# Luna attention and SMELU: first keys as float32 and cast on chip, values ahead of queries, softmax groups by halves of the heads

## The chip, the cores and the metric

The kernel runs on one core of a Trainium2 chip, in one launch. The metric is device time in microseconds, the median over runs; 260.56 us is the time before the change (3 runs, 260.14 to 262.5).

A core has five engines with a queue each: TensorE (PE, multiplies matrices into PSUM), VectorE (DVE), ScalarE (ACT), GpSimd (POOL) and SyncE (SP). Transfers are issued from the queues of SyncE, ScalarE and GpSimd. In this kernel those of GpSimd turn float32 in memory into bf16 on the way, those of the other two move data as it is, or transpose it.

## The reference

```python
batch, n_heads, seq, head_dim = (8, 8, 576, 64); n_pack = 32
def sm_attn(qq, kk, vv):
    s = scale * np.matmul(qq, kk.transpose(0, 1, 3, 2))      # scale = 1/sqrt(64)
    s = s - np.max(s, axis=-1, keepdims=True)
    a = np.exp(s)
    a = a / (np.sum(a, axis=-1, keepdims=True) + 1e-09)
    return np.matmul(a, vv)
p_packed = sm_attn(p, k, v)               # 32 packed rows for each head
out = sm_attn(q, p_packed, p_packed)      # 576 rows attend to the 32 packed rows
x = out, heads side by side               # (4608, 512)
h = x @ w_in                              # w_in (512, 2048)
g = where(h >= 1, h, where(h <= -1, 0, (h + 1)**2 / 4))
result = g @ w_out                        # w_out (2048, 512), float32
```

## The kernel before, in words

The work goes batch by batch, eight blocks. For a block, keys (`k`), queries (`q`) and values (`v`) are loaded as bf16 by GpSimd's queue (`load`, L251 to L255), two buffers of each. The stages of `attention`, by the names of its functions and tiles:

- `trans`: the tokens of four heads are transposed by 12 matmuls into `tp` (PSUM), and copied to `kT` or `qT` (SBUF). Blocks 3 to 7 use `turned` instead: a transposing transfer on SyncE's queue (L481).
- `scores`: `sp` = keys times packed queries for four heads, and `ex`, its exponential, on ScalarE. Two halves `i` = 0, 1.
- `packed`: `pk` = values times `ex` (48 small matmuls) and sums of `ex` (12), copied to `ppT`, in two layouts since a head is needed on the upper or lower 64 partitions; `rs` is the reciprocal of the sums.
- `weights(g)`: for a group `g` of four heads, `s2` = packed keys times queries, `eT` its exponential, `sm` the sums over the packed rows (a matmul with a block of ones), `ln` and `rc` (their reciprocal by logarithm and exponential) on ScalarE, and `A`, the normalised weights, on VectorE.
- `mk(f)`: `M` = packed values times a quarter of `w_in` (`mp` in PSUM), so that `h` below is `A` times `M`, without the attention's output being formed.
- `hidden_tile`: `h`, 4 matmuls each for 16 slices of the hidden layer; three steps on ScalarE and VectorE make the activation (`x`, and `hT` in bf16).
- `out_tile`: for two blocks at a time, nine tiles of 128 tokens; a tile is 16 matmuls (`o`) of `hT` with `w_out`, a copy to `ob`, and stores by SyncE's queue. Tiles 0 to 3 of a pair need the first block alone, so their `o` can be done while the second block's softmax is on its way.

Before the change a group `g` is every second head (`h` = 2a + g), so a group needs both halves of the queries. In the last tile of all (`done_last`) ScalarE and VectorE each copy half of the columns of one PSUM tile, and each half is stored by its own queue.

The order of instructions isn't written by hand. `Plan` (L31 to L172) replays the kernel at build time with a table of costs (`C`, L12 to L16): each task has engines that may do it, a cost, a key (its priority) and tasks that it depends on; `both` lets the planner choose between VectorE and ScalarE; PSUM tiles are rooms of which `W` has three and `O` two. The engine that can start first gets its next task, and the instructions are issued in that order. Each engine then runs its list in order and waits on semaphores. Until the first output tile has begun, TensorE is given dummy matmuls on a tile of zeros (L618, `idle`) wherever the planner sees it without work, each counted as `DW / 2400` us. Transfers of GpSimd's queue stand in the order in which they are added: keys in halves, queries, values, then four pairs of weight slices, then block 1, the rest of `p`, and from block 2 on as buffers come free.

Of the kernel before, what the change touches and what calls it, by code (L numbers as in the profile page):

```python
# [11 lines left out]
C = dict(load=3.0, w_in=2.65, w_out=2.55, out=9.0, p=3.1, land=1.9, xt=5.0, xland=2.5,  # L12
         tpp=0.06, tp=0.042, sc=0.034, pk=1.18, s2=0.25, sm=0.245, M=0.345, h=0.49, o=0.217, switch=0.05,
         pTc=0.1, Tca=1.12, Tcd=0.76, Tc2a=0.64, Tc2d=0.457, ex=0.82, ppTa=0.26, ppTd=0.293, rs=0.18, eT=0.74, ln=0.65, rc=0.68, A=0.82,
# [16 lines left out]
class Plan:  # L31
# [8 lines left out]
    def __init__(self, rooms):  # L40
        self.tasks, self.now, self.mode = [], {e: 0.0 for e in self.ENGINES}, 0
        self.rooms = {nm: [0.0] * n for nm, n in rooms.items()}
        self.count = {nm: 0 for nm in rooms}
        self.now["DMA"] = 2.85
        self.log = []
# [130 lines left out]
def kernel(  # L176
# [10 lines left out]
    nc = tc.nc  # L187
# [28 lines left out]
    nc.scalar.preload_act_table_set("natural_log_exp_and_others")  # L216

# [22 lines left out]
    nc.sync.dma_start(p_raw, p_v[:, :PB * 2])  # L240
# [10 lines left out]
    def load(nm, b, hs):  # L251
        if (nm, b) not in tok:
            tok[nm, b] = stg.tile([TP, H, NC, D], bf16, tag=nm, name=nm)
        nc.gpsimd.dma_start(tok[nm, b][:, hs].rearrange("p h c d -> p h (c d)"),  # L254
                            SRC[nm][b, hs].rearrange("h (p c) d -> p h (c d)", c=NC))  # L255
# [9 lines left out]
    nc.vector.memset(pT, 0.0)  # L265
    HS = [slice(0, 4), slice(4, 8)]
# [5 lines left out]
    def add_load(nm, b, parts=1, deps=()):  # L272
        for i, hs in enumerate([ALL] if parts == 1 else HS):
            L[nm, b, i] = add(DMA, C["load"] / parts, -1, deps, lambda nm=nm, b=b, hs=hs: load(nm, b, hs))
        if parts == 1:
            L[nm, b, 1] = L[nm, b, 0]
# [62 lines left out]

    def attention(b, key):  # L340
# [9 lines left out]
        def trans(nm, i, dst, prev):  # L350
# [11 lines left out]
            split = 2 if b == 0 else 1  # L362
            t = add(PE, C["tp"] * 12, ky, [L[nm, b, i]] + prev, mm, takes="W", readers=split, mode=0)
            if split == 1:
                def cp(eng):
                    w = 4 * E * TP
                    copy(dst()[:, i, :w].rearrange("p (j c) -> p j c", j=X), box["tp"][:, :, :w // 2])(eng)
                return t, [both(cp, C["Tca"], C["Tcd"], ky, [t], frees=t)]
            res = []
            for j in range(X):  # L370
                def cp(eng, j=j):
                    w = 2 * E * TP
                    copy(dst()[:, i, j * w:(j + 1) * w], box["tp"][:, j, :w])(eng)
                res.append(both(cp, C["Tc2a"], C["Tc2d"], ky, [t], frees=t))
            return t, res

        def scores(i, deps):
            box, ky = {}, key["sc" + str(i)]

            def mm():  # L380
                sp = box["sp"] = wide([P, 2, FW], f32, "sp")
                for j in range(2):
                    for e in range(E):
                        for g in range(G):
                            h, o = G * (2 * i + j) + g, (e * G + g) * X * NP
                            w = ((G * j + g) * E + e) * TP
                            nc.tensor.matmul(sp[:, j, o:o + X * NP], kT()[:, i, w:w + P],  # L387
                                             pT[:, b, h].rearrange("p x n -> p (x n)"), start=True, stop=True)

            def ev(eng):  # L390
                nc.scalar.activation(ex().rearrange("p e g x a n -> p a (e g x) n")[:, 2 * i:2 * i + 2],  # L391
                                     box["sp"][:TP, :, :E * G * X * NP].rearrange("p j (c n) -> p j c n", n=NP),
                                     AF.Exp, scale=scale)
            t = add(PE, C["sc"] * 12, ky, deps, mm, takes="W", readers=1, mode=0)
            return t, add(ACT, C["ex"], ky, [t] + old("pk"), ev, frees=t)

        def packed(deps):
            box, ky = {}, key["pk"]

            def mm():  # L400
# [3 lines left out]
                for a in range(Q):  # L404
                    for c in range(NC):
                        for g in range(G):
                            nc.tensor.matmul(v_[g * D:(g + 1) * D, a], vt[:, G * a + g, c], ex_[:, c // X, g, c % X, a],  # L407
                                             start=(c == 0), stop=(c == NC - 1))
# [5 lines left out]
            t = add(PE, C["pk"], ky, [L["v", b, 0]] + deps, mm, takes="W", readers=4, mode=1)  # L414
# [8 lines left out]
        def pp_of(x, g, a):  # L423
            return ppT()[x * D:(x + 1) * D, 0 if x == g else 1, a]

        def weights(g, deps, r):
            box, ky, km = {}, key["s2" + str(g)], key["sm" + str(g)]

            def mm():
                s2 = box["s2"] = wide([P, X, FW], f32, "s2")  # L430
                for a in range(Q):
                    for x in range(X):
                        nc.tensor.matmul(s2[a * NP:(a + 1) * NP, x, :HALF], pp_of(x, g, a),  # L433
                                         qT()[x * D:(x + 1) * D, a // 2, (G * (a % 2) + g) * E * TP:][:, :E * TP], start=True, stop=True)
# [31 lines left out]
        def mk(f, deps):  # L466
            box, ky = {}, key["M" + str(f)]

            def mm():
                mp = box["mp"] = wide([P, G, FW], f32, "mp")  # L470
                for a in range(Q):
                    for g in range(G):
                        nc.tensor.matmul(mp[a * NP:(a + 1) * NP, g], pp_of(g, g, a),  # L473
                                         w_in_sb[g * D:(g + 1) * D, a, f * FW:(f + 1) * FW], start=True, stop=True)
            t = add(PE, C["M"], ky, deps + [L["in", f]], mm, takes="W", readers=1, mode=2)
            return t, both(lambda eng: copy(M()[:, :, f * FW:(f + 1) * FW], box["mp"])(eng),
                           C["Mca"], C["Mcd"], ky, [t] + K.get((b - 2, "h"), []), frees=t)
# [19 lines left out]
        ws = [weights(g, pc + qc0 + qc1, r) for g in range(G)]  # L497
# [51 lines left out]
    def out_tile(pr, i):  # L549
        box, prev = {}, []  # L550
        bs = range(2 * pr + i * P // S, 2 * pr + ((i + 1) * P - 1) // S + 1)

        def step(fi):
            if fi == 0:
                box["o"] = psO.tile([P, d_model], f32, tag="o", name="o")
            nc.tensor.matmul(box["o"], hT[:, fi, i * P:(i + 1) * P], w_out_sb[:, fi, :], start=(fi == 0), stop=(fi == KF - 1))  # L556
# [7 lines left out]
        def done_last(eng):  # L564

            w = d_model // 2
            for j, (eng, queue) in enumerate(((ACT, nc.scalar), (DVE, nc.sync))):
                ob = ops.tile([P, w], f32, tag="ob" + str(j), name="ob" + str(j), bufs=1)
                copy(ob, box["o"][:, j * w:(j + 1) * w])(eng)
                for a, n, dst in out_rows(pr, i):  # L570
                    queue.dma_start(dst[:, j * w:(j + 1) * w], ob[a:a + n])
# [7 lines left out]
        both(done if 2 * pr + 2 < B or i + 1 < NT else done_last, C["oba"], C["obd"], b_key(pr, i), prev, frees=owner, takes="ob", holds=C["out"])  # L579
# [69 lines left out]
```

## Time and profile before

| | |
|---|---|
| median of the runs | 260.56 us |
| profiled execution, time | 261.9 us |
| its span | 259.8 us |
| granted TensorE clock, mean | 0.995 |
| busy: TensorE, ScalarE, VectorE | 247.3, 185.9, 173.3 us |
| busy: GpSimd | 27.4 us |
| moved by the DMA engines | 34.40 MB, mean 132 GB/s |
| GpSimd's queue (q0), SyncE's queue (q1) | 18.55 MB, 15.34 MB |

The span is from the first to the last instruction of one execution; its time has what lies around it too. Bytes are counted as they are written, so a load that casts counts half of what it reads. A busy share is a mean over stages with different limits: the first 23 us are loads and block 0's softmax, then blocks overlap until about 226 us, and the last 29 us are `o` alone.

### The profile page before, as it was taken

The numbers are of one execution on the slowest core, as the hardware profiler recorded it, in microseconds if no ns is written. First come the engines' busy times: TensorE is split into PE (matmuls) and PEld (weight loads), VectorE is DVE, ScalarE is ACT, GpSimd is POOL, SyncE is SP. The second block draws the span as 40 slices with busy tenths as digits, with TensorE's granted clock in tenths as the row PEclk, the third lists the DMA queues.
The fourth block names the chain that finished last, engine by engine and source line by source line (L and its number), as shares of the span: only waits on it lengthen the run. The fifth ranks groups of instructions, "written<-read, shape, count | busy, mean of one in ns | idle before, by whom it ended". The sixth has DMA issues, their size and how long they took to land.

```text
span 259.8 us, 5951 instructions
## 1 busy us (share of the span) xinstructions
PE 247.3 (95%) x2432; PEld 145.7 (56%) x2466; DVE 173.3 (67%) x299; ACT 185.9 (72%) x303; POOL 27.4 (11%) x40
## 2 busy tenths in 40 slices
PE   7999989999998999999999999999999999999992
PEld 5978546467545655654655565555554465644440
DVE  5135989678988997999748974897268876940000
ACT  3447886789898898999949895998559775841110
POOL 8522312102100300210201000000000000000000
PEclk9999999999999999999999999999999999999997
DMA  7999999999999999999999995301222111133223
GB/s 108 187 204 206 208 202 195 217 230 194 139 148 196 148 226 183 178 164 179 161 165 141 154 217 122 76 19 31 43 81 43 42 43 40 40 78 85 59 63 82
DMA packets 54764, 34.40 MB, mean 132 GB/s; under 512 B 27473, under 2 KB 50257, under 8 KB 54737
## 3 DMA queue, kind: packets, MB, share of 16 engines
q0 software_dynamic: 24608, 18.55, 51.7%
q1 hardware_dynamic: 29968, 15.34, 33.4%
q8 instruction: 19, 0.31, 0.5%
q10 hardware_dynamic: 160, 0.13, 0.2%
q14 instruction: 9, 0.07, 0.1%
HBM read 37.22 MB, written 9.44 MB: 180 GB/s over the span
## 4 chain that ended last, share of the span: by engine, by line
PE 70%; DMA 20%; ACT 5%; issue 2%; POOL 1%; SPq 0%; DVE 0%; POOLq 0%
PE o L556 41%; PE h L513 17%; DMA k<-in_k_dram 8%; DMA kT<-k 6%; DMA w_in_sb<-in_moe_w_in_dram 5%; PE mp L473 2%; PE pk L407 2%; ACT eT L438 2%; PE sp L387 2%; PE tp L359 2%; ACT x L518 1%; ACT M L307 1%; PE pk L412 1%; PE s L433 1%; DMA out_dram<-ob 1%
## 5 line engine op out<-in xcount | busy, mean ns | idle before, releaser
L556 PE MATMUL o<-w_out_sb,hT 128*128 128x512 bf16 x542 | 136.2, 379 | 1.3 <-issue 0.5
L528 DVE SCALAR_TENSOR_TENSOR hT<-x 128x576 bf16<-128x576 f32 x128 | 94.2, 756 | 22.3 <-PE o L556 16.4
L518 ACT ACTIVATE x<-h 128x576 f32<-128x576 f32 x128 | 78.9, 658 | 11.3 <-PE h L513 7.4
L556 PEld LDWEIGHTS <-hT 128*128 128x128 bf16 x576 | 54.6, 98 | 54.4 <-issue 4.3
L513 PE MATMUL h<-A,M 128*128 128x288 bf16 x512 | 78.5, 286 | 1.5 <-ACT M L307 0.7
L513 PEld LDWEIGHTS <-M 128*128 128x128 bf16 x512 | 48.4, 98 | 25.6 <-issue 3.6
L523 DVE TENSOR_SCALAR x<-x 128x576 f32<-128x576 f32 x102 | 47.0, 463 | 13.7 <-ACT x L518 12.8
L307 ACT COPY ob<-o 128x512 f32<-128x512 f32 (+1 forms) x24 | 13.8, 576 | 36.7 <-PE o L556 36.1
L307 DVE COPY ob<-o 128x512 f32<-128x512 f32 (+1 forms) x13 | 8.7, 668 | 27.2 <-ACT ob L307 24.9
L307 ACT CAST M<-mp 128x1024 bf16<-128x1024 f32 x26 | 25.9, 1011 | 0.0
L618 PE MATMUL o<-zeros 128*128 128x256 bf16 x138 | 18.3, 285 | 1.2 <-DVE zeros L242 1.2
L525 ACT ACTIVATE x<-x 128x576 f32<-128x576 f32 x26 | 17.5, 684 | 0.5
L618 PEld LDWEIGHTS <-zeros 128*128 128x128 bf16 x138 | 13.5, 102 | 3.7 <-DVE zeros L242 1.2
L454 DVE SCALAR_TENSOR_TENSOR A<-eT,rs,rc 128x576 bf16<-128x576 bf16 x16 | 13.0, 814 | 2.5 <-ACT rc L451 2.3
L391 ACT ACTIVATE ex<-sp 96x768 bf16<-96x768 f32 x16 | 12.9, 815 | 2.3 <-PE sp L387 2.3
L254 POOL DMA_DIRECT2D k<-in_k_dram x9 | 7.4, 821 | 67.8 <-issue 28.7
L473 PE MATMUL mp<-w_in_sb,ppT 64*32 64x512 bf16 x256 | 13.1, 384 | 0.9 <-ACT x L518 0.4
L438 ACT ACTIVATE eT<-s,rs 128x576 bf16<-128x576 f32 x16 | 11.7, 744 | 1.1 <-PE s L433 0.9
L447 ACT ACTIVATE ln<-sm 128x576 f32<-128x576 f32 x16 | 10.5, 657 | 1.2 <-PE sm L443 1.1
L451 ACT ACTIVATE rc<-ln 128x576 f32<-128x576 f32 x16 | 10.9, 684 | 0.5
L387 PEld LDWEIGHTS <-kT 128*128 128x128 bf16 x192 | 7.6, 98 | 3.3 <-DMA kT<-k 1.3
L307 ACT CAST ppT<-pk 64x128 bf16<-64x128 f32 (+1 forms) x21 | 5.4, 259 | 5.6 <-PE pk L412 4.5
(44 smaller groups left out, 116.2 us busy)
## 6 DMA issues: line engine op xcount, KB each, us to landing
q<-in_q_dram POOLq DMA_DIRECT2D x8, 576.0 KB, 15.3
v<-in_v_dram POOLq DMA_DIRECT2D x8, 576.0 KB, 16.1
out_dram<-ob SPq DMA_DIRECT2D x23, 192.0 KB, 2.8
k<-in_k_dram POOLq DMA_DIRECT2D x7, 576.0 KB, 14.7
out_dram<-ob SPq DMA_DIRECT2D x24, 128.0 KB, 2.4
w_in_sb<-in_moe_w_in_dram POOLq DMA_DIRECT2D x4, 512.0 KB, 18.3
w_out_sb<-in_moe_w_out_dram POOLq DMA_DIRECT2D x4, 512.0 KB, 19.1
out_dram<-ob SPq DMA_DIRECT2D x23, 64.0 KB, 2.2
```

What stands on the lines that cost most here:

```text
L307: return lambda eng: nc.vector.tensor_copy(out_, in_) if eng == DVE else nc.scalar.copy(out_, in_)
L391: nc.scalar.activation(ex().rearrange("p e g x a n -> p a (e g x) n")[:, 2 * i:2 * i + 2], box["sp"][:TP, :, :E * G * X * NP].rearrange("p ...
L438: nc.scalar.activation(box["eT"], box["s2"][:, :, :HALF], AF.Exp, scale=rs()[:, g, 1:])
L454: nc.vector.scalar_tensor_tensor(A()[:, g], box["eT"], rs()[:, g, :1], box["rc"], ALU.mult, ALU.mult)
L473: nc.tensor.matmul(mp[a * NP:(a + 1) * NP, g], pp_of(g, g, a), w_in_sb[g * D:(g + 1) * D, a, f * FW:(f + 1) * FW], start=True, stop=True)
L513: nc.tensor.matmul(h[:, hf, :HALF], T[b, "M"][:, g, fi * P:(fi + 1) * P], T[b, "A"][:, g, hf], start=(g == 0), stop=(g == G - 1))
L518: nc.scalar.activation(box["x"], box["h"][:, :, :HALF], AF.Prelu, bias=-1.0, alpha=0.5)
L523: nc.vector.tensor_scalar(x, x, 1.0, 0.0, ALU.add, ALU.max)
L525: nc.scalar.activation(x, x, AF.Relu, bias=1.0)
L528: nc.vector.scalar_tensor_tensor(hT[:, fi, col:col + S].rearrange("p (a t) -> p a t", a=2), box["x"], 1.0, box["x"], ALU.min, ALU.mult)
L556: nc.tensor.matmul(box["o"], hT[:, fi, i * P:(i + 1) * P], w_out_sb[:, fi, :], start=(fi == 0), stop=(fi == KF - 1))
L618: plan.run(lambda: nc.tensor.matmul(o[:, :DW], zeros[:, :P], zeros[:, :DW], start=True, stop=True))
```

## The change

Four parts, and the planner's table is adapted to them:

1. Block 0's keys are loaded as float32 by SyncE's queue into the memory of `hT`, which isn't in use yet, and cast to bf16 by ScalarE and VectorE (`cast_k0`). `p_raw` goes to ScalarE's queue. On GpSimd's queue the values come first, then the queries in two halves.
2. The copies of block 0's `kT` and `qT` are no longer split in two; the second layout of `ppT` is copied from the first in SBUF, by VectorE, instead of from PSUM.
3. A group of the softmax is now half of the heads, 4g to 4g+3 (`head`), so group `g` needs the half `g` of the queries alone. `scores` writes its tile in the order in which `ex` is kept.
4. The last output tile is summed in two PSUM tiles of 256 columns; each is copied by one engine, and each of two queues then stores whole rows of it.

```diff
-C = dict(load=3.0, w_in=2.65, ...
+C = dict(load=3.0, first=3.8, w_in=2.65, ...
-        self.now["DMA"] = 2.85
+        self.now["DMA"] = 1.3
...
-    nc.scalar.preload_act_table_set("natural_log_exp_and_others")
...
-    nc.sync.dma_start(p_raw, p_v[:, :PB * 2])
+    nc.scalar.dma_start(p_raw, p_v[:, :PB * 2])
+    nc.scalar.preload_act_table_set("natural_log_exp_and_others")
...
-        nc.gpsimd.dma_start(tok[nm, b][:, hs].rearrange("p h c d -> p h (c d)"),
-                            SRC[nm][b, hs].rearrange("h (p c) d -> p h (c d)", c=NC))
+        src = SRC[nm][b, hs].rearrange("h (p c) d -> p h (c d)", c=NC)
+        if (nm, b) == ("k", 0):
+            nc.sync.dma_start(k_raw[:, hs], src)
+        else:
+            nc.gpsimd.dma_start(tok[nm, b][:, hs].rearrange("p h c d -> p h (c d)"), src)
...
+    k_raw = hT.rearrange("p f t -> p (f t)").bitcast(f32)[:TP, :H * NC * D].rearrange("p (h c) -> p h c", h=H)
...
     def first_loads():
         for hs in HS:
             load("k", 0, hs)
+        load("v", 0, ALL)
         make_identity(nc, ident)
...
-    add_load("q", 0)
-    add_load("v", 0)
+    L["v", 0, 0] = L["v", 0, 1] = add(DMA, C["first"], -1, (), lambda: None)
+    add_load("q", 0, 2, cost="first")
...
+    def head(g, a):
+        return 4 * g + (a ^ g)
+
+    def cast_k0(i):
+        res = []
+        for j, e in enumerate((ACT, DVE)):
+            hs = slice(4 * i + 2 * j, 4 * i + 2 * j + 2)
+            res.append(add(e, C["kc"], -2.5, [L["k", 0, i]],
+                           lambda eng, hs=hs: copy(tok["k", 0][:, hs].rearrange("p h c d -> p h (c d)"), k_raw[:, hs])(eng)))
+        return res
...
     scores:
+                for e in range(E):
+                    o = sp[:, e * X * Q * NP:(e + 1) * X * Q * NP].rearrange("p (x a n) -> p x a n", x=X, a=Q)
+                    for a in range(Q):
+                        h = head(i, a)
+                        w = (h % 4 * E + e) * TP
+                        nc.tensor.matmul(o[:, :, a], kT()[:, i, w:w + P], pT[:, b, h], start=True, stop=True)
...
     packed:
-            res = [both(lambda eng: copy(ppT()[:, 0], box["v"])(eng), C["ppTa"], C["ppTd"], ky, [t] + war, frees=t)]
-            for x in range(X):
-                res.append(both(lambda eng, x=x: copy(ppT()[x * D:(x + 1) * D, 1], box["v"][(1 - x) * D:(2 - x) * D])(eng),
-                                C["ppTa"], C["ppTd"], ky, [t] + war, frees=t))
+            c = both(lambda eng: copy(ppT()[:, 0], box["v"])(eng), C["ppTa"], C["ppTd"], ky, [t] + war, frees=t)
+            res = [c] + [add(DVE, C["ppx"], ky, [c], lambda eng, x=x: copy(ppT()[x * D:(x + 1) * D, 1], ppT()[(1 - x) * D:(2 - x) * D, 0])(eng))
+                         for x in range(X)]
...
     mk:
+            if (b, f) == (0, 0):
+                return t, add(DVE, C["Mcd"], ky, [t], cp, frees=t)
...
-        ws = [weights(g, pc + qc0 + qc1, r) for g in range(G)]
+        ws = [weights(g, pc + (qc0, qc1)[g], r) for g in range(G)]
...
     out_tile:
+        end = 2 * pr + 2 == B and i + 1 == NT
+        w = d_model // 2
+        def spare():
+            box["o2"] = wide([P, w], f32, "o2")
...
+            for o, cs in [(box["o"][:, :w], slice(w)), (box["o2"], slice(w, d_model))] if end else [(box["o"], slice(d_model))]:
+                nc.tensor.matmul(o, hT[:, fi, i * P:(i + 1) * P], w_out_sb[:, fi, cs], start=(fi == 0), stop=(fi == KF - 1))
...
     done_last:
-            for j, (eng, queue) in enumerate(((ACT, nc.scalar), (DVE, nc.sync))):
-                ob = ops.tile([P, w], f32, tag="ob" + str(j), name="ob" + str(j), bufs=1)
-                copy(ob, box["o"][:, j * w:(j + 1) * w])(eng)
-                for a, n, dst in out_rows(pr, i):
-                    queue.dma_start(dst[:, j * w:(j + 1) * w], ob[a:a + n])
+            ob = ops.tile([P, d_model], f32, tag="ob", name="ob")
+            copy(ob[:, :w], box["o"][:, :w])(ACT)
+            copy(ob[:, w:], box["o2"])(DVE)
+            for (a, n, dst), queue in zip(out_rows(pr, i), (nc.sync, nc.scalar)):
+                queue.dma_start(dst, ob[a:a + n])
```

More of the change, by code (lines that the diff above doesn't have):

```diff
@@ L270, with add_load @@
     L = {}
-    def add_load(nm, b, parts=1, deps=()):
+    def add_load(nm, b, parts=1, deps=(), cost="load"):
         for i, hs in enumerate([ALL] if parts == 1 else HS):
-            L[nm, b, i] = add(DMA, C["load"] / parts, -1, deps, lambda nm=nm, b=b, hs=hs: load(nm, b, hs))
+            L[nm, b, i] = add(DMA, C[cost] / parts, -1, deps, lambda nm=nm, b=b, hs=hs: load(nm, b, hs))
         if parts == 1:
@@ L361, in mm, with cp @@
                                                 ident[:TP, :TP])
[L362 to L375, printed above, removed]
+            t = add(PE, C["tp"] * 12, ky, (cast_k0(i) if (nm, b) == ("k", 0) else [L[nm, b, i]]) + prev, mm, takes="W", readers=1, mode=0)
+            def cp(eng):
+                w = 4 * E * TP
+                copy(dst()[:, i, :w].rearrange("p (j c) -> p j c", j=X), box["tp"][:, :, :w // 2])(eng)
+            return t, [both(cp, C["Tca"], C["Tcd"], ky, [t], frees=t)]
         def scores(i, deps):
@@ L578, in out_tile @@
                 owner = t
-        both(done if 2 * pr + 2 < B or i + 1 < NT else done_last, C["oba"], C["obd"], b_key(pr, i), prev, frees=owner, takes="ob", holds=C["out"])
+        both(done_last if end else done, C["oba"], C["obd"], b_key(pr, i), prev, frees=owner, takes="ob", holds=C["out"])
     def b_key(pr, i):
```

51 lines of the change are left out of this document (25 added, 26 removed).

## The prediction

> **What bounds the kernel now.** I began with the page: the span, the slices, the DMA queues, and the group of dummy matmuls on `zeros`.
>
> ```profile
> span 259.8 us, 5951 instructions
> DMA  7999999999999999999999995301222111133223
> q0 software_dynamic: 24608, 18.55, 51.7%
> q10 hardware_dynamic: 160, 0.13, 0.2%
> L618 PE MATMUL o<-zeros 128*128 128x256 bf16 x138 | 18.3, 285 | 1.2 <-DVE zeros L242 1.2
> ```
>
> Of TensorE's matmuls 138 are filler. The DMA row reads 9 from the second slice to the 24th, and its slices are 6.5 us: for some 150 us the transfers may set the pace as well. So I asked whom TensorE waits for, and for the chain of waits.
>
> ```profile
> PE o L618 <- DVE zeros L242: 1.2, 1, 1.2
> PE tp L359 <- DMA k<-in_k_dram: 1.0, 1, 1.0
> PE sp L387 <- DMA kT<-k: 0.8, 1, 0.8
> ```
>
> ```profile
> 17.75 20.72 DMA k<-in_k_dram
> 38.52 0.68 PE tp L359 x12
> 67.97 15.81 DMA kT<-k
> 83.82 0.52 PE sp L387 x12
> 85.54 0.43 PE o L556 x2
> ```
>
> These name the two gates. Block 1's keys let the transposes go at 38.52, after 0.97 us of waiting. At 83.82 block 3's second transposed keys let the second `sp` go, after 0.79 us. Of the first 84 us of the chain these two transfers are 36.5; behind the second gate the chain has none until the stores. The windows give the rate of the transfers, and TensorE's idle time behind the second gate.
>
> ```profile
> 1.00:2.00 1.00, 0.81 (x4) 0.58 (x5) 0.63 (x2) 1.00 (x1) 0.70 (x1) 1.00 0.04 10
> 2.00:3.00 1.00, 1.00 (x7) 0.73 (x5) 1.00 (x1) 0.02 (x1) 0.98 (x3) 1.00 0.74 131
> 3.00:4.00 1.00, 0.94 (x5) 0.33 (x3) 0.76 (x9) 0.00 (x0) 0.95 (x2) 1.00 0.81 101
> 15.00:38.00 23.00, 21.84 (x248) 14.61 (x247) 16.23 (x27) 17.34 (x29) 6.46 (x8) 1.00 1.25 205
> 52.00:54.00 2.00, 2.00 (x17) 0.81 (x16) 1.29 (x3) 1.94 (x5) 0.00 (x0) 1.00 1.22 274
> 84.00:255.00 171.00, 168.93 (x1485) 93.38 (x1505) 113.59 (x193) 123.52 (x204) 7.19 (x9) 1.00 0.67 108
> ```
>
> The last two columns are the DMA share and GB/s. Loads run at a flat 205 GB/s of bf16 written, and from 84 to 255 us TensorE idles only 2.1 of 171 us. So up to 84 us the transfer stream paces the kernel and TensorE has filler to give away; from there it is TensorE alone, and whatever is gained at the second gate reaches the end.
>
> **The first transfers.** Now GpSimd's queue casts keys, queries and values in turn; the timeline has the issues, with what ended the queue's waits in brackets.
>
> ```profile
> 0.74 0.47 SPq L240 DMA_DIRECT2D p_raw<-in_p_dram  x1
> 1.30 1.46 POOL L254 DMA_DIRECT2D k<-in_k_dram  x2 [0.86 <-POOLq L633]
> 11.51 0.75 POOL L280 DMA_DIRECT2D w_in_sb<-in_moe_w_in_dram  x1 [2.18 <-DMA q<-in_q_dram]
> 15.65 0.74 POOL L282 DMA_DIRECT2D w_out_sb<-in_moe_w_out_dram  x1 [3.40 <-DMA v<-in_v_dram]
> 17.75 0.79 POOL L254 DMA_DIRECT2D k<-in_k_dram  x1 [1.36 <-DMA w_in_sb<-in_moe_w_in_dram]
> ```
>
> Block 0's queries are down at about 11.5, the values at 15.6. By 4.0 us the windows hold 242 KB; 131 of them are `p_raw` (128 x 256 floats), so the casting loads have moved 111 KB, 0.55 us at 205: their stream in effect starts at 3.45. `p_raw`, issued by SyncE at 0.74, has its first bytes at about 1.9. Keys issued at 0.74 by SyncE should flow from 1.9 too; `p_raw`, now issued by ScalarE at the same moment, is in their way for 0.65 us (131 KB at share 0.74, less its ramp). Start 2.55: 0.9 us earlier.
>
> What float32 keys cost, 1.18 MB written in place of 0.59, is not in the trace. Dear end: the mix of loads and float32 stores at 52 us ran at 274, so they need at most 4.3 us, against 2.9 cast: 1.4 lost. Cheap end: the q10 row (1 KB stores) is 0.2% x 259.8 x 16 / 160 = 52 ns a packet, q0 is 87 ns for 754 bytes; keys would take 768 x 78 ns / 16 = 3.7 us of engine time against 4.2, and at the share of 1.25 that is 0.4 gained. The packets are the nearer row, being one kind of transfer; I count 0.3. The stream moves by 1.2 us (from -0.5 to +1.3), and all behind it: weights, block 1, block 3.
>
> The Trainium skill ("DMA: Bandwidth & Descriptors", "Issuing engines are not separate DMA queues") says that transfers issued by several engines share the same 16 DMA engines, so that issuing from more of them saves only the issuing time. By that rule the stream gains the 0.56 us between the two issues, and the sum would end at 259.4; the windows, with a slow ramp up to 4 us, speak for more.
>
> The cast is new work: twice 96x768 on ScalarE and on VectorE. Nearest rows:
>
> ```profile
> L523 DVE TENSOR_SCALAR x<-x 128x576 f32<-128x576 f32 x102 | 47.0, 463 | 13.7 <-ACT x L518 12.8
> L391 ACT ACTIVATE ex<-sp 96x768 bf16<-96x768 f32 x16 | 12.9, 815 | 2.3 <-PE sp L387 2.3
> ```
>
> That is 0.82 on ScalarE, between 0.6 (the 463 ns scaled by 768/576) and 1.0 on VectorE. Behind the casts on VectorE stand the copies to `kT`, on which `sp` waits; on ScalarE the two `ex`. The keys lie in `hT` until then, whose first `hT` write comes only after the softmax. `p_raw` at the head of ScalarE's queue holds up its table load and the copies to `pT` by the 0.47 of the issue, under fillers; without these it would cost the 0.47.
>
> **TensorE's order.** The listing of both orders has 138 fillers now and 120 changed. A filler takes 115 ns (3.44 us for 30), so 18 are 2.07 us. From the timeline:
>
> ```profile
> 9.06 0.68 PE L359 MATMUL tp<-ident,k 96*128 96x96 bf16 x12
> 19.80 3.44 PE L618 MATMUL o<-zeros 128*128 128x256 bf16 x30
> 15.41 0.94 PE L407 MATMUL pk<-ex,v 96*64 96x32 bf16 x48
> ```
>
> Ahead of `pk` stand 21 fillers and 24 query transposes fewer (two of the 0.68 us), so it comes at 15.41 - 2.4 - 1.3 = 11.7; the values, second in the stream where the queries were, are down by 11.5 - 1.2 = 10.3. The second key transposes come six fillers earlier, at 9.06 - 0.7 = 8.4. Keys that have the DMA engines to themselves need 3.7 / 1.25 = 3.0 us from 2.55 and are down at 5.5; if they share evenly with the values from 3.45 on, at 7.7. Cast (0.85 more), that is 6.4 to 8.6: a stall of some tenths at most.
>
> Do the 2.07 us reach the end? At the second gate both orders have done the same real work, but for one `o` more in the changed one (96 for 95; 0.43/2 = 0.22 us). TensorE was ready at 83.82 - 0.79 = 83.03 and would now be at 83.03 - 2.07 + 0.22 = 81.2, or 80.2 if the first gate's 0.97 goes too. The gate, if it follows the stream, opens at 83.8 - 1.2 = 82.6. So it decides: the wait grows to 1.4 us or more, swallowing the startup's stall, and the gain is 1.2 + 0.22 = 1.4.
>
> The gate hangs on SyncE's queue in the timeline: block 3's first transposed keys, then a store, then transposed queries, then the second keys.
>
> ```profile
> 62.32 5.59 SPq L481 DMA_TRANSPOSE qT<-q  x1
> 67.97 8.43 SPq L481 DMA_TRANSPOSE kT<-k  x1
> ```
>
> In the changed order the store's tile (o number 64) stands after the second `sp` of block 2 instead of before, so the 62.32 issue may not move. Then loads run longer without transposes beside them; the total of transfers is the same and I keep 1.2. Should it hold the gate, the gain there is 0.2.
>
> **Groups, copies, PSUM.** Halves of the heads change no instruction count in `sp`, `pk`, `s` or `mp`: same shapes, other heads. In block 0 the first `s` needs half the queries, which the order has used. Unsplit `kT` and `qT` copies are on VectorE behind the casts, under filler. `ppT` is now one copy from PSUM and two from SBUF on VectorE, where three came from PSUM, mostly on ScalarE. In a later block:
>
> ```profile
> 111.27 1.14 PE L513 MATMUL h<-A,M 128*128 128x288 bf16 x8
> 111.91 0.55 ACT L307 CAST ppT<-pk 128x128 bf16<-128x128 f32 x2
> 112.04 0.76 DVE L528 SCALAR_TENSOR_TENSOR hT<-x 128x576 bf16<-128x576 f32 x1 [0.19 <-ACT x L525]
> 114.29 0.32 PE L433 MATMUL s<-qT,ppT 64*32 64x288 bf16 x8
> ```
>
> From the end of `pk` to `s` there are 2.9 us; the changed order puts 8 `h` and 10 `o` there, about 3.1. The first of these copies, half of 0.55, is the one that stays; two more from SBUF at no more than that make 0.8, with hand-overs and the reciprocal some 1.2 us, and leave room for two `hT` ahead. Zero, and ScalarE, which sets the block's softmax, has less to do.
>
> **The last tile.** 32 matmuls of 256 columns take 32 x 0.115 = 3.68 for 16 x 0.215 = 3.44: +0.24.
>
> ```profile
> 255.04 0.37 ACT L307 COPY ob<-o 128x256 f32<-128x256 f32 x1 [2.82 <-PE o L556]
> 255.45 0.42 DVE L307 COPY ob<-o 128x256 f32<-128x256 f32 x1 [24.86 <-ACT ob L307]
> 255.90 0.86 SPq L571 DMA_DIRECT2D out_dram<-ob  x2
> ```
>
> The end of the timeline shows it: VectorE waited for ScalarE's copy of the same PSUM tile; with two tiles it starts 0.41 earlier. One store a queue for two saves 0.43 on SyncE. Both queues now wait for both copies, which costs nothing since VectorE's ends last anyway. Against that, the stores are twice as wide:
>
> ```profile
> out_dram<-ob SPq DMA_DIRECT2D x23, 192.0 KB, 2.8
> out_dram<-ob SPq DMA_DIRECT2D x1, 96.0 KB, 2.0
> ```
>
> The 2.8 is a median over busy stretches and an upper end: the tail is between -0.6 and +0.2; I take -0.4, nearer to the quiet end.
>
> **Sum.** The profiled execution took 261.9 (259.8 span and 2.1 around it). Gains 1.2 + 0.22 + 0.4 = 1.8 give 260.1 there; from the median 260.56 it is 258.7.
>
> **Rivals.** A: the gate opens with TensorE. Two queues together may fill the DMA engines better than the first 4 us show, and fewer loads beside the transposes shorten those 8.43 us. Then the fillers count in full with both waits: 2.07 + 0.97 + 0.4 = 3.4, at 257.2. For it: transposes and loads share badly (15.81 us for one). Against: nothing removes transfers.
>
> B: the stream doesn't move. VectorE's casts of float32 in SBUF hold up GpSimd's descriptors by up to 2 x 0.6 us, or the store holds the transposed queries: gain 0.22 + 0.4, at 259.9. The 102 `x<-x` of the same kind speak against it: issues beside them last 0.74 to 0.79. The Trainium skill ("SBUF — State Buffer", "SBUF: two separate sides") describes this lock between VectorE's two-port modes and descriptors written by GpSimd; these rows show little of it.
>
> C: float32 keys at the 274 row: the stream is 0.5 later and 0.5 us more at the gate is lost to a stalled start, at 260.9.
>
> D, slower: `ppT` behind VectorE's queue. After 84 us nothing absorbs a wait; if the two SBUF copies come behind more than two `hT` (0.76 each), the 3.1 us are exceeded, and `s` and `mp` wait with all that follows on TensorE. One `hT` too many in each of the five blocks left is 3.8 us, an `hT` and an `x` (0.46) too many 6.1: with 258.7, 262.5 to 264.8; I put 263.6. It decides from 1.9 us of queue ahead of the copies. For it: the copies move to the engine that also has every `hT`. Against: VectorE is busy 114 of the 171 us.
>
> **How the numbers follow.** Forecast 0.44 (own range 257.8 to 259.6), A 0.33, B 0.07, C 0.06, D 0.10. Over 1% faster, about what a measurement of this kernel can tell from no change, is under 257.95: all of A and a fifth of the forecast, 0.42. Over 263.2 are D and a little of C: 0.11. The rest is 0.47. The range takes in A with 0.4 below it and C: 256.8 to 261.0.
>
> **What would show it.** Fillers 120; values landing before 11 us; the queue's waits at 15.65 and 17.75 about a microsecond sooner; the first `h` 2 us sooner, near 21; the second `sp` of block 3 near 82.6 with a wait of over 1 us; no new idle after; VectorE's last copy starting with ScalarE's. Wrong, if that `sp` goes at 81 without a wait (A), after 83.5 (B, C), or if idle grows between 84 and 255 (D).

## The result, and the profile after

The changed kernel takes 262.95 us (20 runs, 262.1 to 264.24), beside 261.02 for the kernel before on the same chip (20 runs, 260.14 to 262.72): a ratio of 1.006, 95% interval 1.0042 to 1.0078. It is slower by 0.6%, where 258.7 was forecast and 261.0 was the upper end of the range. The profiled execution took 264.24 us, the longest of the 20; the one of the kernel before, 261.9, was 0.9 above its median. Lines of the two profiles therefore stand further apart than the medians.

The page first: the span, the transfers by slices (6.56 us each), and the fillers.

```profile
span 262.4 us, 5980 instructions
DMA  6999999999999999999999995111121111123223
GB/s 168 206 206 207 207 204 195 223 218 202 192 104 115 154 202 163 178 162 182 179 156 172 208 208 104 42 40 41 42 80 42 41 40 42 40 65 85 62 70 80
L644 PE MATMUL o<-zeros 128*128 128x256 bf16 x120 | 19.2, 315 | 1.2 <-DVE zeros L241 1.2
```

There are 18 fillers fewer, as forecast, but they are busy for 19.2 us instead of 18.3: 315 ns each where 285 were. Next, whom TensorE waited for (total us, times, longest):

```profile
PE tpp L325 <- DVE p_nat L322: 2.8, 1, 2.8
PE s L445 <- ACT eT L450: 1.4, 1, 1.4
PE sp L400 <- DMA kT<-k: 0.4, 1, 0.4
```

The first gate (block 1's keys, 0.97 us) is gone, the second has shrunk to 0.4, and two waits are there that the kernel before did not have. The one of 1.4 us lies between the two gates, where TensorE has block 1's second `s` to do and ScalarE has copies of `pT` ahead of the `eT` on which it waits:

```profile
52.81 0.32 PE L445 MATMUL s<-qT,ppT 64*32 64x288 bf16 x8 [1.35 <-ACT eT L450]
```

The other, 2.8 us, stands at the very start: `tpp`, the transposes of `p_nat`. The timeline shows the chain behind it (start, duration, what it is, and in brackets the idle time ahead with what ended it):

```profile
0.74 0.46 ACTq L238 DMA_DIRECT2D p_raw<-in_p_dram  x1
6.42 0.29 DVE L322 CAST p_nat<-p_raw 128x256 bf16<-128x256 f32 x1 [2.34 <-DMA p_raw<-in_p_dram]
6.77 0.40 PE L325 MATMUL tpp<-ident,p_nat 128*128 128x128 bf16 x2 [2.84 <-DVE p_nat L322]
6.96 4.90 PE L644 MATMUL o<-zeros 128*128 128x256 bf16 x22
8.19 1.73 ACT L313 CAST k<-hT 96x768 bf16<-96x768 f32 x2
11.65 1.14 PE L379 MATMUL tp<-ident,k 96*128 96x96 bf16 x12
26.31 1.63 PE L530 MATMUL h<-A,M 128*128 128x288 bf16 x12
86.89 0.52 PE L400 MATMUL sp<-pT,kT 128*128 128x64 bf16 x12 [0.43 <-DMA kT<-k]
```

The same places before:

```profile
4.34 0.34 PE L319 MATMUL tpp<-ident,p_nat 128*128 128x128 bf16 x2 [0.40 <-DVE p_nat L316]
4.51 3.22 PE L618 MATMUL o<-zeros 128*128 128x256 bf16 x28
7.57 0.68 PE L359 MATMUL tp<-ident,k 96*128 96x96 bf16 x12
23.08 1.63 PE L513 MATMUL h<-A,M 128*128 128x288 bf16 x12
```

`p_raw`, 131 KB, issued at the same 0.74 as before, landed at 6.4 instead of 3.05. The trace also holds the single transfers of each queue, with start and length. Those of `p_raw` run from 2.95 to 5.42, among the float32 keys of SyncE's queue (1.79 to 8.03); before they ran alone, from 1.87 to 2.72. GpSimd's values, though issued at 1.30, move nothing until 7.21, so they took no part in `p_raw`'s lateness; what held them back no run shows. So `tpp` is 2.43 us late, and behind the idling the 22 fillers take 223 ns each (28 took 115 ns before) and the 12 key transposes 1.14 us in place of 0.68: TensorE runs at half speed up to about 12.6. The first `h` comes at 26.31, not at 23.08, and not at the 21 forecast. From the second `sp` of block 3 to the end of the span it is 262.4 - 86.89 = 175.5 us, before 259.8 - 83.82 = 176.0. The whole loss lies ahead of that `sp`.

The stream of transfers itself moved a little. GpSimd's queue waits for the landings of the values, now second in the stream (the queries had that place, until 11.51), and of `w_in`'s first quarter (before: until 17.75):

```profile
11.68 0.75 POOL L286 DMA_DIRECT2D w_out_sb<-in_moe_w_out_dram  x1 [3.88 <-DMA v<-in_v_dram]
16.98 0.79 POOL L257 DMA_DIRECT2D k<-in_k_dram  x1 [1.66 <-DMA w_in_sb<-in_moe_w_in_dram]
```

And the tail:

```profile
257.81 0.37 ACT L313 COPY ob<-o 128x256 f32<-128x256 f32 x1 [2.80 <-PE o L580]
257.93 0.42 DVE L313 COPY ob<-o 128x256 f32<-128x256 f32 x1 [24.55 <-PE o L580]
258.42 0.32 SPq L594 DMA_DIRECT2D out_dram<-ob  x1
258.43 0.38 ACTq L594 DMA_DIRECT2D out_dram<-ob  x1
```

VectorE's copy starts 0.12 us after ScalarE's (0.41 before). From ScalarE's copy to the end of the span it is 262.4 - 257.81 = 4.6 us, before 259.8 - 255.04 = 4.8.

### The profile page after: what moved, and what is told of

It reads as the page before. It is cut to its first block, busy times and chain, and to the rows that moved or that the text cites. A ratio compares the mean times of both kernels' runs of the same rounds, so it can differ in the third digit from the quotient of the medians.

```text
span 262.4 us, 5980 instructions
## 1 busy us (share of the span) xinstructions
PE 251.0 (96%) x2464; PEld 146.9 (56%) x2464; DVE 175.9 (67%) x306; ACT 184.4 (70%) x296; POOL 26.4 (10%) x39
## 4 chain that ended last, share of the span: by engine, by line
PE 83%; DMA 9%; DVE 4%; ACT 3%; issue 0%; SPq 0%; DVEq 0%
PE o L580 44%; PE h L530 20%; DMA kT<-k 7%; PE o L644 5%; PE mp L487 3%; PE pk L419 3%; PE tp L379 3%; DMA p_raw<-in_p_dram 2%; PE sp L400 2%; DVE hT L545 2%; PE sm L455 1%; PE s L445 1%; PE pk L424 1%; DVE x L540 1%; ACT x L535 1%; ACT pT L313 1%
## 5 line engine op out<-in xcount | busy, mean ns | idle before, releaser
L580 PE MATMUL o<-w_out_sb,hT 128*128 128x512 bf16 (+1 forms) x592 | 146.2, 374 | 0.8 <-DVE hT L545 0.6
L580 PEld LDWEIGHTS <-hT 128*128 128x128 bf16 x592 | 55.9, 98 | 53.6 <-issue 4.7
L540 DVE TENSOR_SCALAR x<-x 128x576 f32<-128x576 f32 x92 | 42.0, 459 | 12.5 <-ACT x L535 11.5
L313 ACT COPY ob<-o 128x512 f32<-128x512 f32 (+1 forms) x27 | 15.5, 578 | 38.1 <-PE o L580 37.7
L542 ACT ACTIVATE x<-x 128x576 f32<-128x576 f32 x36 | 24.4, 685 | 0.5
L313 DVE COPY ob<-o 128x512 f32<-128x512 f32 (+1 forms) x10 | 6.5, 662 | 26.0 <-PE o L580 26.0
L313 ACT CAST M<-mp 128x1024 bf16<-128x1024 f32 x23 | 23.2, 1014 | 0.0
L644 PE MATMUL o<-zeros 128*128 128x256 bf16 x120 | 19.2, 315 | 1.2 <-DVE zeros L241 1.2
L257 POOL DMA_DIRECT2D k<-in_k_dram x7 | 5.4, 776 | 71.0 <-DMA kT<-k 31.4
L313 DVE CAST M<-mp 128x1024 bf16<-128x1024 f32 x9 | 11.0, 1220 | 2.0 <-PE mp L487 1.9
```

Source lines behind the costliest of these rows:

```text
L313: return lambda eng: nc.vector.tensor_copy(out_, in_) if eng == DVE else nc.scalar.copy(out_, in_)
L540: nc.vector.tensor_scalar(x, x, 1.0, 0.0, ALU.add, ALU.max)
L542: nc.scalar.activation(x, x, AF.Relu, bias=1.0)
L580: nc.tensor.matmul(o, hT[:, fi, i * P:(i + 1) * P], w_out_sb[:, fi, cs], start=(fi == 0), stop=(fi == KF - 1))
L644: plan.run(lambda: nc.tensor.matmul(o[:, :DW], zeros[:, :P], zeros[:, :DW], start=True, stop=True))
```

## The experiments

The theory: the first loads come late to TensorE because they share the DMA engines with one another; TensorE idles, loses its clock, and nothing behind it takes the lateness back. The rivals: the new softmax groups, copies or tail cost time; or the float32 keys and their casts do, on any queue. Ratios are to the kernel before on the same chip (261.42 for 1 to 4, 261.11 for 5 to 7, 261.30 for 8 to 10).

**1. `p_raw` back to the head of SyncE's queue.**

```diff
-    nc.scalar.dma_start(p_raw, p_v[:, :PB * 2])
+    nc.sync.dma_start(p_raw, p_v[:, :PB * 2])
```

> The changed kernel with one line undone: p_raw is issued by SyncE, ahead of the float32 keys, in place of by ScalarE beside them; the instruction order of every compute engine is the same. Theory T (p_raw shares the DMA engines with the keys, lands at 6.4 instead of 3.05, TensorE idles and then runs its fillers at half speed): p_raw lands near 3.1, the first tpp goes near 4.4, the 22 fillers behind it take 2.5 us instead of 4.9, the first h is near 21.3 instead of 26.3, and what is left is the forecast's sum: 258.5 to 259.5 us. Rival R (the new groups, the ppT copies or the values-first order cost time wherever p_raw stands): the first h may move, but the time stays at 261.5 to 263. Rival S (float32 keys load the transfer stream, so the second gate, the second sp of block 3, stays near 84): 260 to 261.

263.78 us, ratio 1.009 (1.0056 to 1.0124): no better than the change. The expectation missed, and the timeline says why:

```profile
4.34 0.40 PE L325 MATMUL tpp<-ident,p_nat 128*128 128x128 bf16 x2 [0.40 <-DVE p_nat L322]
8.38 1.15 PE L644 MATMUL o<-zeros 128*128 128x256 bf16 x9
11.22 0.83 ACT L313 CAST k<-hT 96x768 bf16<-96x768 f32 x1 [3.42 <-DMA hT<-in_k_dram]
12.11 0.95 PE L379 MATMUL tp<-ident,k 96*128 96x96 bf16 x12 [2.58 <-ACT k L313]
13.28 0.85 PE L400 MATMUL sp<-pT,kT 128*128 128x64 bf16 x12
```

`tpp` is back at 4.34, but the keys' second half, issued half a microsecond later, now lands at 11.20 instead of 9.07. TensorE idles 2.58 us there and is slow again (`sp` 0.85 for 0.51). The first `h` is at 26.42, as late as in the change. So `p_raw`'s place alone was not the cause: whichever of the two is served last is the late one. No run issues `p_raw` from ScalarE's queue with nothing beside it, so that queue itself isn't excluded as a part of the 6.40. Its stores speak against it: in the changed kernel 192 KB took 2.6 us from ScalarE's queue and a median of 2.4 from SyncE's.

**2. 24 more fillers ahead of `tpp`,** the change otherwise as it is: TensorE no longer idles while `p_raw` is late.

```diff
                 nc.vector.tensor_copy(p_nat[:, 2 * b0:2 * b1], p_raw)
+                for _ in range(24):
+                    nc.tensor.matmul(o[:, :DW], zeros[:, :P], zeros[:, :DW], start=True, stop=True)
```

> The changed kernel with 24 more fillers put directly before the first tpp, nothing else moved: TensorE then works through the wait for p_raw, which lands as late as before. It tells the wait from the clock. Theory T with a cold clock: tpp still at 6.7 to 7.0, but the 22 fillers behind it take 2.5 us instead of 4.9 and the 12 key transposes 0.68 instead of 1.14, so the first h comes 2.5 us earlier than 26.3, near 23.7, and the time falls by 1.5 to 2.5 us, to 260.5 to 261.5. If the fillers were slow for another reason (their operands, contention), they stay at 4.9 us and the time stays at 263 or rises.

261.41 us, ratio 0.9994 (0.9971 to 1.0016): 1.5 us under the changed kernel, with more work and the same transfers (`p_raw` at 6.12).

```profile
7.44 0.28 PE L327 MATMUL tpp<-ident,p_nat 128*128 128x128 bf16 x2
7.55 2.56 PE L646 MATMUL o<-zeros 128*128 128x256 bf16 x22
24.14 1.63 PE L532 MATMUL h<-A,M 128*128 128x288 bf16 x12
```

`tpp` is even 0.67 us later than in the change, but the 22 fillers behind it take 2.56 us in place of 4.90, and the first `h` is 2.2 us sooner. Nearly all of the 0.6% comes back although `tpp` is as late as ever: most of the loss of time came from the clock.

**3. The kernel before with `p_raw` late,** issued by GpSimd behind the two key halves.

```diff
-    nc.sync.dma_start(p_raw, p_v[:, :PB * 2])
...
+        nc.gpsimd.dma_start(p_raw, p_v[:, :PB * 2])
```

> The kernel before with only p_raw moved: issued by GpSimd behind block 0's keys, so that it lands at about 7; order of all compute engines as before. Theory T: this alone makes the kernel before slow: tpp waits for about 3.5 us, the fillers behind it run at half speed, the first h comes at 27 to 29 instead of 23, and the time rises by 3 to 5 us, to 264 to 266. Rival (the loss belongs to the float32 keys or the new groups): within 0.5 us of the kernel before.

265.68 us, ratio 1.0156 (1.0117 to 1.0195), the time as expected. The waits have `PE tpp` with 4.2 us; the first `h` is 6.0 us late and the second `sp` of block 3, at 87.52, 3.7 us. So part is taken back in the old order, whose two gates had waits of 1.8 us to give. A late `p_raw` is enough to make the kernel before slow, with nothing else of the change in it.

**4. The change without its first loads:** keys, then queries, then values on GpSimd's casting queue, `p_raw` on SyncE's; groups, copies and the last tile as changed.

```diff
-        if (nm, b) == ("k", 0):
-            nc.sync.dma_start(k_raw[:, hs], src)
...
-    nc.scalar.dma_start(p_raw, p_v[:, :PB * 2])
+    nc.sync.dma_start(p_raw, p_v[:, :PB * 2])
...
```

> The changed kernel without its first part: keys, queries, values in the old order on GpSimd's casting queue, p_raw on SyncE; the new groups, the ppT copies from SBUF, the unsplit copies and the last tile in two PSUM tiles stay. Theory T: these cost nothing, and the tail gains 0.2 to 0.4: 260 to 261 us, with TensorE idle less than 2 us between 84 us and the last tile. Rival R (the groups or the ppT copies cost): 262 to 264, with new waits of s or mp after 84 us.

260.30 us, ratio 0.995 (0.9929 to 0.9971): better than both kernels. The windows show TensorE without a gap (busy us first) from 84 to 220 us:

```profile
84.00:220.00 136.00, 136.00 (x1329) 76.64 (x1327) 105.49 (x183) 110.27 (x180) 6.62 (x8) 1.00 0.81 116
```

The rival that puts the loss on groups, copies or tail falls. With other loads the planner also made another order for TensorE: the `s` that waits 1.35 us in the changed kernel waits for nothing here.

**5. Values held until the first key half is down** (from experiment 1).

```diff
-        load("v", 0, ALL)
         make_identity(nc, ident)
+        nc.gpsimd.tensor_copy(held, k_raw[:, 0, :16])
+        load("v", 0, ALL)
```

> The first experiment's kernel (p_raw on SyncE's queue ahead of the float32 keys), and GpSimd makes the identity first and then reads 16 elements of the first key half before it issues the values, so that p_raw and the keys don't share the 16 DMA engines with the values. If sharing made the keys late: p_raw lands near 3.1, the key halves near 4.6 and 6.1 in place of 6.96 and 11.20 (1.5 us for a half, as between the two key halves of the kernel before), the second key transposes wait for no cast, the values land at 10 to 10.8 and w_in's first part at 16.5 to 17.2 (the stream loses part of its 0.8 us), first `h` at 22 to 23.5, span 257.5 to 259, time 259 to 261: 3 us under the first experiment. If float32 keys on SyncE's queue are slow by themselves: the second half stays behind 9, the wait at the second key transposes stays above 1 us, the values are later still, and the time is 264 or more.

263.28 us, ratio 1.0086 (1.0055 to 1.0118), with runs from 261.53 to 264.87. The transfers answered in part, the time not at all:

```profile
8.30 0.83 ACT L315 CAST k<-hT 96x768 bf16<-96x768 f32 x1 [1.02 <-DMA hT<-in_k_dram]
9.19 0.68 PE L381 MATMUL tp<-ident,k 96*128 96x96 bf16 x12 [0.19 <-ACT k L315]
13.39 0.94 PE L421 MATMUL pk<-ex,v 96*64 96x32 bf16 x48 [0.85 <-DMA v<-in_v_dram]
16.27 0.68 PE L381 MATMUL tp<-ident,q 96*128 96x96 bf16 x12 [1.43 <-DMA q<-in_q_dram]
```

Without the values beside them the keys' second half lands at 8.28 instead of 11.20, so sharing cost it 2.9 us. But 6.1 was expected: the keys are slow even alone (first half 6.43). And the values, issued at 7.00, and the queries behind them are late instead. It separates the landings, and as a repair it fails.

**6. 24 more fillers ahead of the second key transposes** (from experiment 1; the keys stay late).

```diff
                 tp = box["tp"] = wide([P, X, 1024], bf16, "tp")
+                if (nm, b, i) == ("k", 0, 1):
+                    warm()                  # 24 matmuls on zeros
```

> The first experiment's kernel with 24 more filler matmuls ahead of the second half of the first key transposes, where TensorE idled 2.9 us; the transfers are as they were (second key half near 11.2). If the time lost there is mostly TensorE's slow clock after the idling: the wait shrinks to under 0.5 us, the score matmuls of the first block take 0.5 instead of 0.85 us, first `h` comes 1 to 2 us sooner than 26.4, and the time is 261.3 to 262.5 in place of 263.8. If it is the lateness of the keys' second half alone, fillers change nothing: 263.3 to 264.3.

261.7 us, ratio 1.0027 (1.0006 to 1.0048), first `h` at 24.49, `sp` 0.51: as the clock's theory had it. The second place where idling cost the clock is shown as the first was in experiment 2.

**7. Experiment 4 with the values ahead of the queries,** the queries by halves.

```diff
-    add_load("q", 0)
     add_load("v", 0)
+    add_load("q", 0, 2)
```

> The fourth experiment's kernel (keys on GpSimd's casting queue, p_raw on SyncE's queue) with the first values ahead of the first queries, and the queries by halves, as in the change. If the order of values and queries is worth little by itself: 259.9 to 260.7, as the fourth (260.3). If the queries, later by the time of the values, hold up the first block's second matmuls and M: 261 to 262.5, with a wait of the query transposes or of s2 for q.

260.30 us, ratio 0.9974 (0.9952 to 0.9995). The first `h` is at 21.71, 1.95 us sooner than in experiment 4, and the time is the same within its interval. The lead is spent before the second gate, where the second `sp` goes only 0.32 us sooner (82.52 for 82.84). TensorE's order was planned anew here too, and in it the `s` waits for `eT` as in the changed kernel, and as in every kernel here with the values first:

```profile
49.01 0.32 PE L442 MATMUL s<-qT,ppT 64*32 64x288 bf16 x8 [1.35 <-ACT eT L447]
```

That is most of the 1.63 us lost on the way. Whether the early start would pay in an order without this wait no run shows.

**8. Float32 keys on GpSimd's queue,** ahead of the values and still without a cast in the transfer (from experiment 1).

```diff
-            nc.sync.dma_start(k_raw[:, hs], src)
+            nc.gpsimd.dma_start(k_raw[:, hs], src)
```

> The first experiment's kernel, but the float32 keys are issued by GpSimd, on the same queue as the values and ahead of them, still without a cast in the transfer; p_raw stays on SyncE's queue. If a queue of its own beside the values is what makes the keys late: the queue serves them in order, the halves land near 6.2 and 8.1 (1.85 us for a half, as where the values were held back), the values at 10.7 to 11.3, no wait at the second key transposes, first `h` at 23 to 24, time 260 to 261.2. If float32 keys and their casts are the loss on any queue: the second key half lands after 9, the second transposes wait over 1 us, time 262.5 or more.

260.66 us, ratio 0.9961 (0.9937 to 0.9985).

```profile
9.56 0.83 ACT L313 CAST k<-hT 96x768 bf16<-96x768 f32 x1 [1.60 <-DMA hT<-in_k_dram]
10.45 0.68 PE L379 MATMUL tp<-ident,k 96*128 96x96 bf16 x12 [0.57 <-ACT k L313]
23.16 1.63 PE L530 MATMUL h<-A,M 128*128 128x288 bf16 x12
```

Neither theory had the landings right: the halves came at 7.10 and 9.54, not at 6.2 and 8.1. Float32 keys do cost on any queue (7.43 with the cast), but the wait is 0.57 us, too short to lose the clock, and the time is that of the first theory. One changed line, the queue that issues the keys, takes 263.78 to 260.66.

**9 and 10. Experiment 7 with TensorE's start made late by 20 and by 42 warm fillers,** the first loads untouched (the edit of experiment 6 with those counts).

> The seventh experiment's kernel (first `h` at 21.71, 260.3 us; transfers as in it) with 20 filler matmuls, 2.3 us, ahead of the second key transposes, so that only TensorE's startup is later and its clock stays fast: first `h` near 24.0. If the gate at 84 us swallows a late startup, as the prediction's second step has it: 260.3. If a late TensorE also makes the later loads late, and there is slack only up to a first `h` of some 23.7 (the time then grew one for one in the kernels so far): 260.3 to 261.

> The same with 42 fillers, 4.8 us: first `h` near 26.4, where the changed kernel has it. If the gate swallows the lateness: 260.3 to 260.8. If the lateness comes through one for one from 23.7 on: 262.5 to 263.3, with the loads of block 4 (k, q, v) issued 1.5 to 3 us later and no wait over 0.5 us at the second `sp` of block 3.

262.37 us, ratio 1.0038 (1.0007 to 1.0068), and 264.73 us, ratio 1.0109 (1.0049 to 1.017). Both are above what was expected of lateness coming through, and above the 260.3 of a gate that swallows it. The profiled spans, 1.8 and 3.3 us over experiment 7's for a first `h` 2.9 and 4.4 later, are nearer to what was expected (some 1 us is taken up, the rest comes through); but experiment 10 has four runs, from 263.4 to 265.7, and the profiled one is the fastest, so by the medians nothing is taken up there. First `h`, second `sp` of block 3 and the issue of block 3's keys, those that the gate waits for, in experiment 7, 9 and 10:

```profile
21.71 1.63 PE L527 MATMUL h<-A,M 128*128 128x288 bf16 x12
39.85 0.77 POOL L255 DMA_DIRECT2D k<-in_k_dram  x1 [6.20 <-PE tp L376]
82.52 0.51 PE L397 MATMUL sp<-pT,kT 128*128 128x64 bf16 x12
```

```profile
24.61 1.63 PE L533 MATMUL h<-A,M 128*128 128x288 bf16 x12
41.78 0.77 POOL L255 DMA_DIRECT2D k<-in_k_dram  x1 [8.22 <-PE tp L382]
84.33 0.51 PE L403 MATMUL sp<-pT,kT 128*128 128x64 bf16 x12
```

```profile
26.11 1.63 PE L533 MATMUL h<-A,M 128*128 128x288 bf16 x12
43.28 0.77 POOL L255 DMA_DIRECT2D k<-in_k_dram  x1 [9.39 <-PE tp L382]
85.83 0.51 PE L403 MATMUL sp<-pT,kT 128*128 128x64 bf16 x12
```

None of these `sp` has a wait in brackets: the gate was open. From experiment 9 to 10 `h`, `sp` and the load move by the same 1.5 us; the load is released by TensorE's own `tp`, the transposes of block 1's keys, which free the buffer. (Block 4's values, released by `pk`, go at 66.05, 67.86 and 69.36.) The gate's transposed keys landed at 81.16, 82.26 and 84.46: a late TensorE makes the gate late too. All kernels together (us); all columns but the last are of the one profiled execution, which in the changed kernel is 1.3 above the median and in experiment 10 1.3 below it:

| | first `h` | second `sp` | span | `sp` to end | median |
|---|---|---|---|---|---|
| before | 23.08 | 83.82 | 259.8 | 176.0 | 261.0 to 261.4 |
| changed | 26.31 | 86.89 | 262.4 | 175.5 | 262.95 |
| 1 | 26.42 | 86.12 | 261.8 | 175.7 | 263.78 |
| 2 | 24.14 | 84.20 | 259.7 | 175.5 | 261.41 |
| 3 | 29.09 | 87.52 | 263.4 | 175.9 | 265.68 |
| 4 | 23.66 | 82.84 | 258.6 | 175.8 | 260.30 |
| 5 | 24.40 | 85.00 | 260.9 | 175.9 | 263.28 |
| 6 | 24.49 | 84.19 | 259.7 | 175.5 | 261.70 |
| 7 | 21.71 | 82.52 | 258.3 | 175.8 | 260.30 |
| 8 | 23.16 | 83.15 | 258.9 | 175.8 | 260.66 |
| 9 | 24.61 | 84.33 | 260.1 | 175.8 | 262.37 |
| 10 | 26.11 | 85.83 | 261.6 | 175.8 | 264.73 |

The fourth numbers column is the same in all twelve within 0.5 us. What differs is when that `sp` goes, and in the changed order it goes 59.7 to 60.8 us after the first `h` (59.2 in experiment 4). The version to keep is experiment 4 (or 7, the same within the intervals): the new groups, copies and last tile with the old first loads.

## Why the prediction was wrong, by its own steps

- **"Under fillers" and "a stall of some tenths at most": the steps that failed.** The prediction let `p_raw` delay the keys, 0.65 us, and never the keys delay `p_raw`; it kept `p_raw`'s landing where it was. Measured: 6.40 for 3.05. The keys alone were put at 5.5 and land at 8.28 (experiment 5, behind `p_raw`); the 3.0 us put for their transfer are 5.4 there (2.45 to 7.86). Beside the values 7.7 was put, and they land at 9.07, or 11.20 behind `p_raw`. Of two queues that both begin by 3 us each is served slower (`p_raw` 2.47 us for 0.85, the keys 6.2 for the 5.4), and the first stage needs all of the small transfer before anything else. The Trainium skill ("DMA: Bandwidth & Descriptors", "Queues, rings and completion order") says that each DMA engine goes round the queues that have work, one packet at a time. The trace agrees for `p_raw` and the keys, whose transfers are mixed between 2.95 and 5.42. The values, issued at 1.30, get no turn before 7.21, which doesn't look like it; why is open.
- **The clock, which no step had.** The prediction counts a stall by its length alone. Of the 5.3 us between the `h` at 26.3 and the forecast 21.0, most can be counted: 2.4 are the later `tpp`, 2.2 the fillers (4.90 for 2.65 in experiment 5) and 0.5 the transposes. Experiments 2 and 6 bring most of it back with fillers alone. The granted clock (after POOL's column) stands at 1.00 in the window of this stage all the same; only the durations of like matmuls show it:

```profile
6.00:12.00 6.00, 5.23 (x29) 3.86 (x30) 1.90 (x5) 2.30 (x4) 2.12 (x4) 1.00 1.26 211
4.53 2.65 PE L646 MATMUL o<-zeros 128*128 128x256 bf16 x22
```

The first row is the changed kernel's window, the second experiment 5's fillers in the same place. The Trainium skill ("TensorE: Matmul & The Clock Gate", "Part 1: The HAM clock gate") says that the clock starts at half and rises after some 3.4 us of sustained work. The kernel before agrees (slow from 1.19 to 4.5); after the idling of the changed kernel it took longer, from 6.77 to about 12.6.
- **The second gate "follows the stream ... swallowing the startup's stall": wrong in the changed order.** The forecast itself had TensorE ready at 81.2 and the gate at 82.6, a slack of 1.4. With the first `h` 5.3 us later than forecast TensorE is ready at 81.2 + 5.3 = 86.5, which is what the trace shows (86.89 less the wait of 0.43). That the way from `h` to the gate comes out right is luck: the first gate's 0.97 went, and the 1.35 us at 52.81, which the sum did not have, came in its place. And the gate does not stand still: experiments 9 and 10 move it by making TensorE late, with the first loads untouched. Block 3's keys, before and changed:

```profile
40.23 0.77 POOL L254 DMA_DIRECT2D k<-in_k_dram  x1 [5.90 <-PE tp L359]
43.77 0.77 POOL L257 DMA_DIRECT2D k<-in_k_dram  x1 [10.11 <-PE tp L379]
```

Lateness of 5.3 less a slack of 1.4, added to the 260.1 forecast for a profiled execution, is 264.0; it took 264.24. Added to 258.7 it is 262.6; the median is 262.95. (The base of 258.7, 260.56 from three runs, is 261.02 with twenty: 0.46 of the miss is that.)
- **The stream's 1.2 us: right in kind, smaller.** `w_in`'s first quarter came 0.77 us sooner; the wait for the values ends at 11.68, where a landing at 10.3 was forecast. It bought nothing, since TensorE was the late one. The 0.3 for cheaper float32 packets is refuted: without a cast the keys' second half lands 2.1 us later on the same queue (experiment 8, 9.54 for 7.43).
- **Groups, copies, one `o` more: zero was right behind the second gate.** From the second `sp` to the end the changed order lost nothing (175.5 for 176.0), and rival D's waits are absent. Ahead of the gate the 1.35 us of `s` are new; they aren't the loss, since experiments 7 and 8 have them too and take 260.3 and 260.66, and they don't come from the groups or copies alone, since experiment 4 is without them. Experiment 4 even gains 0.5%. In it the gate opened at 82.35 in place of 83.78 with the first loads in their old order, which is rival A's case of a gate that opens with TensorE; which edit frees it was not isolated.
- **The tail's 0.4: 0.2 within the span, and perhaps 0.3 outside it.** VectorE's copy starts 0.29 us nearer to ScalarE's; from SyncE's store to the end of the span it is 3.98 us (before 3.90). The 32 narrow matmuls start 109 ns apart in the trace, so they cost 0.04 us, not 0.24. And an execution takes 1.7 to 1.8 us more than its span in all runs of the changed kernel and its variants, 2.1 to 2.2 in those of the kernel before and of experiment 3. The prediction kept 2.1. Which edit saves these 0.3 us was not isolated; they are part of experiment 4's gain of 1.1.
- **Rival C** ended on the right side of its sign (float32 keys dear), but for a small part: on GpSimd's queue float32 keys give 260.66. It is the second queue, beside the values, that costs 3 us in experiment 1.

## What to carry to other kernels

Issuing the first loads from more queues can finish the one that is needed first later (6.40 for 3.05 here), and need not start the others sooner (the values moved from 7.21 on). Order the startup by what the first instruction waits for; the kernels at 260.3 to 260.7 have the small transfer alone on one queue and all the large ones, in the order of need, on one other. Price a stall at the start by what the idling does to the next few microseconds of matmuls, not by its length; a row of fillers longer than planned is the sign of it, and more fillers are a cheap cover. Before a slack is counted on at a later wait, ask whether what ends that wait hangs on the same engine that is late: here the keys behind the gate were loaded when TensorE's transposes of an earlier block had freed their buffer.

## What the runs showed of the hardware that was not expected

- A transfer of 131 KB, issued at the same moment, landed at 3.05 us where the only other loads were issued 0.56 us later by GpSimd, and at 6.40 beside float32 keys of SyncE's queue. Its own transfers took from 1.87 to 2.72 in the one and from 2.95 to 5.42 in the other.
- GpSimd's first load, issued at 1.30 in all three, moved its first bytes at 2.82 us (before), at 4.61 with `p_raw` and the keys on SyncE's queue (experiment 1), and at 7.21 with `p_raw` on ScalarE's and the keys on SyncE's (changed).
- A float32 key half of 590 KB took 1.85 us behind the first one with the DMA engines to itself (6.43 to 8.28), 2.44 ahead of others on GpSimd's queue (7.10 to 9.54) and 4.24 on SyncE's queue beside GpSimd's loads (6.96 to 11.20, experiment 1).
- After 2.7 us of work and 2.8 us of idling, 22 matmuls of 256 columns ran at 223 ns each, where they take 115 to 120 without the idling, while the granted clock of these rows reads 1.00.
